# Half of w_out ahead of all other weight loads, a new order of loads, a weight product by halves, and value blocks on six banks: a fused attention and feed-forward kernel

## The chip, the cores and the metric

The kernel runs on one core of a Trainium2 chip. The metric is the device time of one execution in microseconds (us); the comparison is between medians of several executions. One execution of each kernel was also recorded by the hardware profiler. Its view has the engines TensorE (PE, with its weight loads as PEld), VectorE (DVE), ScalarE (ACT), GpSimd (POOL) and the queue engine SyncE (SP), and the DMA queues that move data between the chip's main memory and its on-chip memory.

## The reference, cut to what matters

Inputs are q, k, v of shape (8 batches, 12 heads, 448 positions, 64), two gain vectors g_q and g_k of 64, and the weights w1, w2 (768 x 1024), w3 (1024 x 1024) and w_out (1024 x 768), all float32.

```python
q_n, k_n = (rmsnorm(q, g_q), rmsnorm(k, g_k))
scores = scale * np.matmul(q_n, k_n.transpose(0, 1, 3, 2))
attn = softmax(scores)                     # written out in the original, with max and sum
attn_out = np.matmul(attn, v)
x = attn_out.transpose(0, 2, 1, 3).reshape(B * S, H * D)     # 3584 x 768
a = x @ w1
b = x @ w2
h = a * b @ w3
return h @ w_out                           # 3584 x 768
```

Nothing nonlinear stands between w3 and w_out, so the kernel forms w34 = w3 @ w_out once and multiplies a * b by it.

## The kernel before, in words

**Blocks.** The 96 heads are taken in 24 blocks of four heads; three blocks make a batch. Each block passes through the same steps. Its q and k (448 KB each) and v (four transfers) are loaded. ACT squares q and k (L414), DVE sums the squares (L421), ACT forms the inverse root (L430, L433), DVE scales (L444). The result is turned by TensorE transposes for the first five blocks (`do_turn`, L1049) and by DMA transposes for the others (L511). Seven score steps (`do_score`, L626) each fill two PSUM banks, and ACT's exponential (L648) empties them into P. Then the value step multiplies P by v and by ones (`start_pv`, `do_pv_main` L711, `do_pv_rest` L690), ACT inverts the sums (L733, L734), and DVE writes the scaled result xT (L753).

**Value blocks.** `pv_size` says whether one block or two are taken together. For two, the 64-row leftovers of both blocks are multiplied as pairs (L690, TensorE in tiles of 64 x 32), and the main part runs in tiles of 128 x 32 (L711). A double needs six PSUM banks in all, two for each of three kinds. It starts when `PV_BANKS` banks are free. The kinds that have both banks at the start take their leftovers first; the leftovers of the others come after the main part. While a double is due, `pe_try` starts no new score and no new pair.

**Pairs.** The feed-forward products and w34 are made by pairs of output tiles in two neighbouring PSUM banks (`Pair`, `do_pass`, L799), in TensorE tiles of 64 x 64: one pass is four matmuls that run side by side. In the first phase the upper 64 rows of each contraction chunk go to one bank and the lower to the other; in the second phase the row halves change places. Between the phases one engine relays a semaphore (`hand_over`), SP until all of w2 is loaded and POOL later, and another pair can run in the gap. At most `MAX_PAIRS` pairs are open. A w34 pair (L838) has 8 + 8 passes and needs one transposed tile of w3 (`do_w3_turn`, L1071) and both halves of w_out; eight such pairs make w34, 128 passes. A pair with w1 (f1a below) is copied to a_sb, one with w2 (f1b) is multiplied on DVE into abT (L882), and output pairs with w34 (f2) are copied to o_sb and stored (L938). The last tile is made by `do_last` (L991) and stored in four parts (L1005).

**Order.** A `Planner` written in the kernel keeps a clock of its own with assumed durations and lays down a fixed order for every engine while the program is built. On the chip each engine runs its list in that order and waits on semaphores. All weights and v, and q and k of blocks 1 to 5, are loaded by POOL in one list, `POOL_ORDER` (L253): w0 to w7 are eighths of w3, o0 and o1 halves of w_out, a0 to a2 thirds of w1, b0 to b2 thirds of w2, q1 to q5 the q and k of a block, v0 to v3 its v. The loads of one queue land in that order. At most eight are under way.

**The start.** `WARM` dummy matmuls (L1226) run first on TensorE. Then comes the product of the gains (`g_product`, L1239), four more dummies, and DVE spreads the gains (L1251, L1252) before it scales q and k of block 0. The planner takes TensorE as free from the value given at L1255.

Of the kernel before, what the change touches and what calls it, by code (L numbers as in the profile page):

```python
# [19 lines left out]
INF = float("inf")  # L20
SEM = 0.05
TO_ENGINE = 0.23
# [173 lines left out]
def kernel(  # L196
# [43 lines left out]

    N_PE_T = 5
    QUAD = 13.0
    WARM = 18
    MAX_PAIRS = 2
    MARGIN = 0.25
    LOW = 2
    PV_BANKS = 4
    SOON = 0
    AHEAD_W3 = 4
    EARLY = 4  # L250
    STOCK = 14
    PACE = 1.7
    POOL_ORDER = (  # L253
        "w0 w1 o0 w2 o1 q1 v0 w3 w4 q2 w5 v1 w6 w7 v2 a0 a1 a2 q3 b0 v3 b1 q4 b2 q5".split()
    )
    ON_POOL = (1, 2, 3, 4, 5)

# [510 lines left out]
    running = [None]  # L768

    class Pair:  # L770
        def __init__(self, name, nk, n, ready, sides, evacuate):
            self.name, self.nk, self.n = name, nk, n
            self.sides, self.evacuate = sides, evacuate
            self.phase, self.pos, self.gap_at = 0, 0, 0.0
            self.needs = ready

        def ready(self):
            return max(self.gap_at, self.needs(self.pos))

    def hand_over(p, mm, t):  # L780

        at = t + 0.23
        e = "SP" if max(w_at["w2"]) == INF else "POOL"
        nop = (nc.sync if e == "SP" else nc.gpsimd).nop()  # L784
        tc.add_manual_dep(
            nop.ins, mm.ins.name, SYNC_DEP, reason="first half of the sums complete"
        )
        free[e] = max(free[e], at)
        p.gap_at = free[e] + 0.15
        p.nop = nop  # L790

    def do_pass(p, t):
        took = pass_us(p.n) + into("n")
        first = None
        for r in range(2):
            z = r ^ p.phase
            lhsT, rhs = p.sides[z](p.pos)
            for h in range(2):
                mm = nc.tensor.matmul(  # L799
                    out=ps_all[64 * h : 64 * h + 64, p.bank + z, 0 : p.n],  # L800
                    lhsT=lhsT[64 * r : 64 * r + 64, 64 * h : 64 * h + 64],
                    rhs=rhs[64 * r : 64 * r + 64],
                    start=(p.phase == 0 and p.pos == 0),
                    stop=(p.phase == 1 and p.pos == p.nk - 1),
                    tile_position=(64 * r, 64 * h),
                    skip_group_check=True,
                )
                first = first or mm
        if p.phase == 1 and p.pos == 0:
            tc.add_manual_dep(  # L810
                first.ins, p.nop.ins.name, SYNC_DEP,
                reason="the other row half takes over the bank",
            )
        p.pos += 1
        running[0] = p
        if p.pos == p.nk:
            running[0] = None
            p.pos = 0
            p.phase += 1
            if p.phase == 1:  # L820
                hand_over(p, mm, t)
            else:
                pairs.remove(p)
                p.evacuate(p, t + took + TO_ENGINE - 0.187)
        return took

    def start_pair(p, z):
# [10 lines left out]
    def w34_pair(fc):  # L838
        def evacuate(p, at):
            z = p.bank  # L840

            def done(e):
                freed(z)(e)
                w34_at.append(e + SEM)

            add(
                None, {"ACT": 0.70, "DVE": 0.89}, -800.0,
                lambda e: copy_on(
                    e,
                    w34s[:, fc, :].rearrange("p (z n) -> p z n", z=2),  # L850
                    ps_all[:, z : z + 2, 0:NH],
                ),
                needs=[lambda: at], done=done,
            )

        side = lambda nh: lambda gc: (
            w3T[:, gc, fc * 128 : (fc + 1) * 128],
            w_outs[:, gc, nh * NH : (nh + 1) * NH],
        )
        return Pair(  # L860
            "w", CF, NH,
            lambda pos: max(w_at["w3T"][fc], w_at["w_out"][pos // (CF // 2)]) + SEM,
            (side(0), side(1)), evacuate,
        )

    a_sb = {}
# [112 lines left out]
    def do_last(t, z):  # L979


        x = last_x[0]
        last_x[0] += 1
        bp, tl = B // 2 - 1, NT - 1
        c0 = tl * 128 + HP * x
        w = NH // 2
        for fi in range(CF):
            for c in range(2):
                for nh in range(2):
                    n0 = nh * NH + c * w  # L990
                    nc.tensor.matmul(  # L991
                        out=ps_all[HP * nh : HP * nh + HP, z + c, 0:w],
                        lhsT=abT[bp][:, fi, c0 : c0 + HP],
                        rhs=w34s[:, fi, n0 : n0 + w],
                        start=(fi == 0), stop=(fi == CF - 1),
                        tile_position=(0, HP * nh), skip_group_check=True,
                    )
        took = 2 * CF * pass_us(w) + into("l")
        bank_at[z] = bank_at[z + 1] = INF
        o_sb = out_pool.tile([128, 2, NH], FP, tag="o_sb", name="o_sb")  # L1000
        ends = []

        def store(nh):
            eng = nc.scalar if nh and x else nc.sync
            eng.dma_start(  # L1005
                out=out_rows(bp, tl, x)[:, nh * NH : (nh + 1) * NH],
                in_=o_sb[HP * nh : HP * nh + HP, 0],
            )

        def done(e):  # L1010
            ends.append(e + SEM)
            if len(ends) == 2:
                for nh in range(2):
                    add(
                        "ACT" if nh and x else "SP", 0.6, -500.0 + nh,
                        lambda nh=nh: store(nh), needs=[lambda: max(ends)],
                    )

        for c, (e, us) in enumerate((("DVE", 0.27), ("ACT", 0.25))):
            add(  # L1020
                e, us, -500.0,
                lambda e=e, c=c: copy_on(
                    e, o_sb[:, 0, c * w : (c + 1) * w], ps_all[:, z + c, 0:w]
                ),
                needs=[lambda: t + took + TO_ENGINE_WIDE - 0.16], done=done,
            )
        return took
# [59 lines left out]
        return took  # L1087

    def next_pair(t):
        if len(pairs) >= MAX_PAIRS:  # L1090
            return None
        return next((p for p in waiting if p.ready() <= t), None)

# [61 lines left out]
    def pe_try(t, r):  # L1155
        idle = idle_banks(r)
        if pv_state:
            took = pv_state[0](t, idle)
            if took is not None:
                pv_state.pop(0)  # L1160
            return took
        size = pv_size(r)
        if mode[0] == "v" and len(idle) >= 1 and size == 1:
            return start_pv(t, 1, idle)
        if size == 2 and len(idle) >= PV_BANKS:
            return start_pv(t, 2, idle)
        two = adjacent(idle)
        score = score_ready(r) and out_scores[0] < 2 and two is not None and size != 2
        hungry = free["ACT"] <= t + 0.3 and out_scores[0] == 0
        if mode[0] == "t":  # L1170
            took = any_turn(t, r, idle, 1)
            if took is not None:
                return took
        if running[0] and running[0].ready() <= r:
            if score and hungry:
                return do_score(t, two)
            return do_pass(running[0], t)
        took = any_turn(t, r, idle, 2)
        if took is not None:
            return took  # L1180
        new = next_pair(r)
        late = [p for p in pairs if p.ready() <= r]
        if score:
            left = [z for z in idle if z not in (two, two + 1)]
            if hungry or late or new is None or adjacent(left) is not None:
                return do_score(t, two)
        if late:
            return do_pass(late[0], t)
        if size == 1 and len(idle) >= 2:
            return start_pv(t, 1, idle)  # L1190
# [17 lines left out]
    with tc.manual_schedule():  # L1208
# [22 lines left out]
        def g_product():  # L1231
# [13 lines left out]
                lhsT=gp_row.rearrange("a x d -> a (x d)"), rhs=ones_row[:, 0:1],  # L1245
                start=True, stop=True,
            )
            warm(4)

        def spread():  # L1250
            nc.vector.tensor_copy(out=g_b, in_=ps_all[:, 6, 0:D])  # L1251
            nc.vector.tensor_copy(out=g_col, in_=ps_all[:, 6, D : D + 1])  # L1252

        warm(WARM)
        free.update(ACT=4.0, DVE=4.0, SP=4.0, POOL=2.3, PE=7.6)  # L1255
        plan.now = plan.moved_to = 2.2
        plan.moving["SP"].append([2.3, 2.6, lambda t: None, 0.086])
        landed[0].update(q=4.5, k=5.4)
# [65 lines left out]
```

## Time and profile before

| | |
|---|---|
| median of 8 runs | 360.79 us (358.59 to 363.62) |
| the profiled execution | 358.59 us |
| its span | 356.8 us |
| time outside the span | 1.8 us |
| ACT, DVE busy | 261.5 us (73%), 207.7 us (58%) |
| first w3 transpose; first score matmul; first value block | 8.44; 11.51; 22.91 us |
| first pass with w1 | 53.09 us |
| start of the last matmuls (L991); last row on TensorE ends | 349.62; 352.45 us |
| granted TensorE clock in the rows | 1.00 throughout |
| bytes moved by DMA | 55.11 MB, mean 154 GB/s |

The profiled execution is the fastest of the eight. Times in the views count from the start of the span. A row of the timeline gives start, duration, engine, source line, operation, operands and count, and in brackets the idle time before it with what ended it. TensorE rows are pipelined: each row's duration contains a tail in which the next row already runs, so the pace is read from the distance between starts.

### The profile page before, as it was taken

The page shows a single profiled execution, that of the slowest core. Times are in us where ns is not written, and L with a number is a line of the kernel's source. Part 1 is how long each engine was busy: PE and PEld are TensorE (multiplying, and loading weights), DVE is VectorE, ACT ScalarE, POOL GpSimd, SP SyncE. Part 2 cuts the span into 40 slices and gives each one's busy share as a digit, 9 for nine tenths or more (in the row PEclk, how much of TensorE's full clock was granted, in tenths as well). Part 3 has the DMA queues.
Part 4 walks back from the last instruction along what each step waited for, and adds up shares of the span by engine and source line. Part 5 has one row for each costly group of instructions (what it writes and reads, how often), then busy time and mean ns, then how long its engine had stood idle before and what let it go on. Part 6 is the DMA issues. An engine that isn't in the chain of part 4 may idle for free.

```text
span 356.8 us, 16164 instructions
## 1 busy us (share of the span) xinstructions
PE 346.2 (97%) x7358; PEld 221.1 (62%) x7358; DVE 207.7 (58%) x293; ACT 261.5 (73%) x375; POOL 75.5 (21%) x132
## 2 busy tenths in 40 slices
PE   8699999999999999999999999999999999999994
PEld 3477656656665666656656565676665567666673
DVE  4278396997998797687579684465353330122200
ACT  4867978979997989988999899778686922222131
POOL 8168261314200505005031040500310000000000
PEclk9999999999999999999999999999999999999999
DMA  8999999679999899976799779961490005100046
GB/s 192 240 265 181 261 269 256 124 170 198 200 201 266 186 241 245 199 124 100 191 240 183 194 78 232 265 69 32 61 204 3 4 2 134 49 4 2 20 128 169
DMA packets 68360, 55.11 MB, mean 154 GB/s; under 512 B 44932, under 2 KB 62244, under 8 KB 68292
## 3 DMA queue, kind: packets, MB, share of 16 engines
q1 hardware_dynamic: 49904, 36.61, 44.6%
q0 software_dynamic: 18016, 16.92, 27.6%
q8 instruction: 57, 0.93, 1.1%
q10 hardware_dynamic: 372, 0.56, 0.5%
q14 instruction: 11, 0.09, 0.1%
HBM read 46.66 MB, written 11.01 MB: 162 GB/s over the span
## 4 chain that ended last, share of the span: by engine, by line
PE 73%; ACT 13%; DMA 6%; DVE 4%; issue 2%; POOL 1%; POOLq 0%; DVEq 0%; SPq 0%
PE ps_all L799 52%; PE ps_all L711 10%; PE ps_all L626 7%; ACT P L648 6%; DMA qk_sb<-in_q_dram 4%; PE ps_all L690 2%; ACT sq L414 2%; DMA qkT<-qks 2%; ACT Pr L648 1%; DVE qks L444 1%; DVE xT L753 1%; DVE ssq L421 1%; PE ps_all L991 1%; ACT w_outs L648 1%; ACT al L433 1%
## 5 line engine op out<-in xcount | busy, mean ns | idle before, releaser
L648 ACT ACTIVATE P<-ps_all 128x896 bf16<-128x896 f32 x120 | 105.1, 919 | 12.0 <-PE ps_all L626 11.8
L363 POOL DMA_DIRECT2D v_sb<-in_v_dram x96 | 57.4, 616 | 172.0 <-PE ps_all L799 118.4
L799 PE MATMUL ps_all<-xT,w2s 64*64 64x448 bf16 x1536 | 89.2, 349 | 0.3 <-ACT P L648 0.3
L799 PE MATMUL ps_all<-xT,w1s 64*64 64x448 bf16 x1536 | 89.4, 349 | 0.0
L799 PE MATMUL ps_all<-w34s,abT 64*64 64x384 bf16 x1728 | 79.3, 323 | 0.4
L882 DVE TENSOR_TENSOR abT<-ps_all,a_sb 128x896 bf16<-128x896 f32 x32 | 34.8, 1089 | 60.0 <-PE ps_all L799 51.4
L799 PEld LDWEIGHTS <-abT 64*64 64x64 bf16 x1728 | 52.4, 107 | 20.3 <-POOLq L784 1.6
L626 PE MATMUL ps_all<-qkT 64*64 64x448 bf16 x672 | 60.8, 352 | 2.9 <-ACT P L648 1.3
L799 PEld LDWEIGHTS <-w2s 64*64 64x64 bf16 x1536 | 47.5, 107 | 25.2 <-issue 1.6
L799 PEld LDWEIGHTS <-w1s 64*64 64x64 bf16 x1536 | 47.1, 107 | 25.1 <-issue 0.4
L421 DVE TENSOR_REDUCE ssq<-sq 128x14 f32<-128x896 f32 (+1 forms) x50 | 51.3, 1042 | 15.9 <-ACT sq L414 15.7
L444 DVE TENSOR_TENSOR qks<-qk_sb,al 128x448 bf16<-128x448 f32 x96 | 55.8, 618 | 4.6 <-ACT al L433 3.7
L414 ACT ACTIVATE sq<-qk_sb 128x896 f32<-128x896 f32 (+1 forms) x50 | 45.1, 918 | 4.8 <-DMA qk_sb<-in_q_dram 4.4
L753 DVE TENSOR_TENSOR xT<-ps_all,r 128x448 bf16<-128x448 f32 x48 | 28.1, 619 | 19.4 <-ACT r L734 18.4
L324 ACT ACTIVATE o_sb<-ps_all 128x768 f32<-128x768 f32 (+1 forms) x22 | 17.0, 771 | 27.8 <-PE ps_all L799 26.2
L324 ACT ACTIVATE a_sb<-ps_all 128x896 bf16<-128x896 f32 x20 | 18.3, 917 | 23.0 <-PE ps_all L799 23.0
L626 PEld LDWEIGHTS <-qkT 64*64 64x64 bf16 x672 | 21.5, 106 | 16.6 <-issue 5.8
L648 ACT ACTIVATE w_outs<-ps_all 128x896 bf16<-128x896 f32 x24 | 21.6, 915 | 8.5 <-PE ps_all L626 8.4
L711 PE MATMUL ps_all<-P,v_sb 128*32 128x448 bf16 x480 | 26.0, 352 | 0.0
L799 PE MATMUL ps_all<-w_outs,w3T 64*64 64x384 bf16 x512 | 24.5, 324 | 0.7 <-ACT P L648 0.5
L711 PEld LDWEIGHTS <-v_sb 128*32 128x32 bf16 x592 | 15.9, 97 | 12.1
L648 ACT ACTIVATE Pr<-ps_all 128x896 bf16<-128x896 f32 x24 | 22.1, 920 | 0.1
(60 smaller groups left out, 213.3 us busy)
## 6 DMA issues: line engine op xcount, KB each, us to landing
out_dram<-o_sb SPq DMA_DIRECT2D x54, 192.0 KB, 3.9
qk_sb<-in_q_dram SPq DMA_DIRECT2D x18, 448.0 KB, 5.0
qk_sb<-in_k_dram SPq DMA_DIRECT2D x18, 448.0 KB, 5.3
v_sb<-in_v_dram POOLq DMA_DIRECT2D x48, 64.0 KB, 4.5
v_sb<-in_v_dram POOLq DMA_DIRECT2D x48, 48.0 KB, 4.5
qk_sb<-in_q_dram POOLq DMA_DIRECT2D x5, 448.0 KB, 9.6
qk_sb<-in_k_dram POOLq DMA_DIRECT2D x5, 448.0 KB, 10.5
w3s<-in_moe_w_dram POOLq DMA_DIRECT2D x8, 256.0 KB, 5.9
```

What stands on the lines that cost most here:

```text
L324: nc.scalar.activation(out=out, in_=in_, func=AF.Copy, scale=1.0 if by is None else by)
L363: nc.gpsimd.dma_start(out=v_bufs[i % 4][p0 : p0 + HP, g::2, 0 : j1 - j0].rearrange("p h j d -> p h (j d)"), in_=src[:, g::2, j0:j1].rearra ...
L414: nc.scalar.activation(out=s["sq", t][:, x0:x1], in_=src[:, t, x0:x1], func=AF.Square)
L421: nc.vector.tensor_reduce(out=s["ssq"][:, t, x0:x1], in_=s["sq", t][:, x0:x1], axis=AX, op=ADD)
L444: nc.vector.tensor_tensor(out=s["qks"][:, t, :, x], in0=src[:, t, x], in1=s["alpha"][:, t, x].unsqueeze(2).broadcast_to([NP, NJ, D]), op=MULT,
L626: nc.tensor.matmul(out=sc[HP * c : HP * c + HP, u, 0:S].rearrange("p (j s) -> p j s", j=NJ), lhsT=qkT[u * D : (u + 1) * D, 1, j, cols], rh ...
L648: lambda: nc.scalar.activation(out=dst, in_=sc[:, :, 0:S], func=AF.Exp),
L690: nc.tensor.matmul(out=ps_all[hd * HALF : (hd + 1) * HALF, banks[x], 0:S], lhsT=(v_bufs[(i + x) % 4][g : g + HP, hd, NF, kind - 1 :: 2] if ...
L711: nc.tensor.matmul(out=ps_all[hd * HALF : (hd + 1) * HALF, z, 0:S], lhsT=value_weights(i, hd, j, kind), rhs=s["P"][:, hd, j, :] if j < NF ...
L753: lambda: nc.vector.tensor_tensor(out=xT[b][:, 2 * m + kind - 1, :], in0=ps, in1=s["r"], op=MULT),
L799: mm = nc.tensor.matmul(out=ps_all[64 * h : 64 * h + 64, p.bank + z, 0 : p.n], lhsT=lhsT[64 * r : 64 * r + 64, 64 * h : 64 * h + 64], rhs= ...
L882: nc.vector.tensor_tensor(out=abT[bp][:, f0 : f0 + 2, odd * S : (odd + 1) * S], in0=ps_all[:, z : z + 2, 0:S], in1=a_sb[b, f0], op=MULT,)
```

## The change

- `POOL_ORDER`: o0 moves from third place to first; w5 to w7 move behind a0 and v1, a1 and a2 come later, b0 ahead of a2, and b2 comes last.
- `Pair` has a list of steps in place of phase and position. With `halves=2` (the first three w34 pairs, `SPLIT`) it does both row assignments on the first half of w_out, then both on the second half, and changes rows twice in place of once.
- Until o1 is counted as landed, up to three pairs may be open (`EARLY_PAIRS`), and a single w3 tile may be transposed at once where two had to be ready.
- A double value block starts on six free banks in place of four.
- A score may break into a running pair earlier while few pairs are waiting (`STARVED`, `HUNGRY`, `ONE`).
- 15 + 1 dummy matmuls in place of 18 + 4; the planner's start value for TensorE goes from 7.6 to 7.2.
- The second half of every store of the last tile is issued by ACT; before, that was so for one of the two.

The engines' lists are laid down anew from all this. In the order of the built kernel, blocks 0, 1, 2 and 5 are taken singly, where before 0 and 5 were; doubles are ten in place of eleven, and every double has all its leftovers ahead of the main part.

```diff
-    WARM = 18
+    WARM = 15
...
-    PV_BANKS = 4
+    PV_BANKS = 6
     SOON = 0
+    STARVED = 6
+    HUNGRY = 0.9
+    ONE = 0
+    SPLIT = 3
+    EARLY_PAIRS = 3
...
-        "w0 w1 o0 w2 o1 q1 v0 w3 w4 q2 w5 v1 w6 w7 v2 a0 a1 a2 q3 b0 v3 b1 q4 b2 q5".split()
+        "o0 w0 w1 w2 o1 q1 v0 w3 w4 q2 a0 v1 w5 w6 v2 w7 a1 v3 q3 b0 a2 b1 q4 q5 b2".split()
...
-            self.phase, self.pos, self.gap_at = 0, 0, 0.0
-            self.needs = ready
+            self.k, self.gap_at, self.needs = 0, 0.0, ready
+            part = nk // halves
+            self.steps = [
+                (x ^ y, part * y + pos)
+                for y in range(halves) for x in range(2) for pos in range(part)
+            ]
...
+        swap, pos = p.steps[p.k]
         for r in range(2):
-            z = r ^ p.phase
-            lhsT, rhs = p.sides[z](p.pos)
+            z = r ^ swap
+            lhsT, rhs = p.sides[z](pos)
...
-            (side(0), side(1)), evacuate,
+            (side(0), side(1)), evacuate, 2 if fc < SPLIT else 1,
...
-            eng = nc.scalar if nh and x else nc.sync
+            eng = nc.scalar if nh else nc.sync
...
-        if len(pairs) >= MAX_PAIRS:
+        if len(pairs) >= (EARLY_PAIRS if w_at["w_out"][1] == INF else MAX_PAIRS):
...
-        hungry = free["ACT"] <= t + 0.3 and out_scores[0] == 0
+        low = sum(p.name != "w" for p in waiting) < STARVED
+        hungry = free["ACT"] <= t + (HUNGRY if low else 0.3) and out_scores[0] <= (
+            ONE if low else 0
+        )
...
-        took = any_turn(t, r, idle, 2)
+        took = any_turn(t, r, idle, 1 if w_at["w_out"][1] == INF else 2)
...
-            warm(4)
+            warm(1)
...
-        free.update(ACT=4.0, DVE=4.0, SP=4.0, POOL=2.3, PE=7.6)
+        free.update(ACT=4.0, DVE=4.0, SP=4.0, POOL=2.3, PE=7.2)
```

More of the change, by code (lines that the diff above doesn't have):

```diff
@@ L770, with __init__, changes @@
     class Pair:
-        def __init__(self, name, nk, n, ready, sides, evacuate):
-            self.name, self.nk, self.n = name, nk, n
+        def __init__(self, name, nk, n, ready, sides, evacuate, halves=1):
+            self.name, self.n = name, n
             self.sides, self.evacuate = sides, evacuate
-            self.phase, self.pos, self.gap_at = 0, 0, 0.0
-            self.needs = ready
-        def ready(self):
-            return max(self.gap_at, self.needs(self.pos))
+            self.k, self.gap_at, self.needs = 0, 0.0, ready
[4 more added lines that the diff above has]
+            ]
+        def ready(self):
+            return max(self.gap_at, self.needs(self.steps[self.k][1]))
+        def changes(self):
+            return 0 < self.k < len(self.steps) and (
+                self.steps[self.k][0] != self.steps[self.k - 1][0]
+            )
     def hand_over(p, mm, t):
@@ L802, in do_pass @@
                     rhs=rhs[64 * r : 64 * r + 64],
-                    start=(p.phase == 0 and p.pos == 0),
-                    stop=(p.phase == 1 and p.pos == p.nk - 1),
+                    start=(p.k == 0), stop=(p.k == len(p.steps) - 1),
                     tile_position=(64 * r, 64 * h),
@@ L808, in do_pass @@
                 first = first or mm
-        if p.phase == 1 and p.pos == 0:
+        if p.changes():
             tc.add_manual_dep(
@@ L813, in do_pass @@
             )
-        p.pos += 1
+        p.k += 1
         running[0] = p
-        if p.pos == p.nk:
+        if p.k == len(p.steps):
             running[0] = None
[L818 to L824, printed above, removed]
+            pairs.remove(p)
+            p.evacuate(p, t + took + TO_ENGINE - 0.187)
+        elif p.changes():
+            running[0] = None
+            hand_over(p, mm, t)
         return took
@@ L1014, in done @@
                     add(
-                        "ACT" if nh and x else "SP", 0.6, -500.0 + nh,
+                        "ACT" if nh else "SP", 0.6, -500.0 + nh,
                         lambda nh=nh: store(nh), needs=[lambda: max(ends)],
@@ L1168, in pe_try @@
         score = score_ready(r) and out_scores[0] < 2 and two is not None and size != 2
-        hungry = free["ACT"] <= t + 0.3 and out_scores[0] == 0
+        low = sum(p.name != "w" for p in waiting) < STARVED
+        hungry = free["ACT"] <= t + (HUNGRY if low else 0.3) and out_scores[0] <= (
+            ONE if low else 0
+        )
         if mode[0] == "t":
```

## The prediction

> **What bounds the kernel now.** I read the page's busy table first, then the chain of waits, then the timeline of TensorE where its starts are further apart than its work.
>
> ```profile
> PE 346.2 (97%) x7358; PEld 221.1 (62%) x7358; DVE 207.7 (58%) x293; ACT 261.5 (73%) x375; POOL 75.5 (21%) x132
> ```
>
> TensorE is near full by this table, but its rows contain pipeline tails, so I count work by pace. In the timeline, 20 matmuls with 448 columns (five passes) start at 236.49 and the next row at 237.44: 0.19 us a pass. A 384-column pass takes 0.1625 (8 passes from 127.33 to 128.76, less the drain of a tile change). Counted so, from the first transpose at 8.44 to the end of the last matmul at 352.45 there are 344.0 us, of which about 327.5 are work. Some 16.5 us are stalls, and only these and the start can give anything. The chain of waits agrees that the tail is pure TensorE and that ACT carries the chain from 55 to 105 us; its row at the start is a load:
>
> ```profile
> 5.49 14.15 DMA qk_sb<-in_q_dram
> ...
> 289.39 58.71 PE ps_all L799 x1324
> ```
>
> After the last double value block TensorE has 58.7 us of feed-forward with no wait. Attention ends early, so whatever TensorE saves earlier reaches the end, as long as attention keeps up. The largest stalls, in the timeline of TensorE:
>
> ```profile
> 7.43 0.20 PE L1239 MATMUL ps_all<-gp_row,ones_row 1*128 1x64 bf16 x1
> ...
> 11.51 0.95 PE L626 MATMUL ps_all<-qkT 64*64 64x448 bf16 x16 [0.79 <-DVE qkT L330]
> 12.92 1.65 PE L799 MATMUL ps_all<-w_outs,w3T 64*64 64x384 bf16 x32 [0.45 <-ACT P L648]
> 14.54 0.38 PE L626 MATMUL ps_all<-qkT 64*64 64x448 bf16 x4
> 15.35 0.38 PE L626 MATMUL ps_all<-qkT 64*64 64x448 bf16 x4 [0.43 <-ACT P L648]
> 16.16 0.38 PE L626 MATMUL ps_all<-qkT 64*64 64x448 bf16 x4 [0.43 <-ACT P L648]
> ```
>
> Four scores are 0.76 us of work and take 1.4 before the first w34 pass at 12.92 (the trace has o0 landing at 12.50). Then three scores take 2.4 us, paced by ACT: only half of w_out is there and nothing else is ready. A second place is at 80 us (whole timeline):
>
> ```profile
> 80.36 1.08 DVE L882 TENSOR_TENSOR abT<-ps_all,a_sb 128x896 bf16<-128x896 f32 x1
> 80.50 1.38 PE L626 MATMUL ps_all<-qkT 64*64 64x448 bf16 x15 [0.32 <-DVE xT L753]
> ...
> 81.89 1.33 PE L799 MATMUL ps_all<-w34s,abT 64*64 64x384 bf16 x28
> ```
>
> The first f2 tile needs the last f1b product, which DVE begins at 80.36 behind xT work; five scores (0.95 us) fill 79.64 to 81.89. The third is every double value block:
>
> ```profile
> 108.54 0.38 PE L690 MATMUL ps_all<-Pr,ones 64*32 64x448 bf16 x8
> ...
> 109.05 1.32 PE L711 MATMUL ps_all<-P,ones 128*32 128x448 bf16 x24
> ...
> 112.56 0.38 PE L690 MATMUL ps_all<-Pr,v_sb 64*32 64x448 bf16 x8
> 112.88 1.33 PE L799 MATMUL ps_all<-xT,w2s 64*64 64x448 bf16 x24
> ```
>
> From 112.56 to 112.88 two leftover passes, 0.19 of work, take 0.32: 0.13 for one change of tile form.
>
> **The change, part by part.** The sums compare the orders of the two built kernels, priced by these rows.
>
> *Start, up to the first value block.* Before, the gain product waits at 7.43 behind 18 dummies; DVE's copies start at 7.68 and its scaling at 7.88. Dummies are 0.217 apart when warm (four from 7.57 to 8.44), so three fewer let the product run near 6.8. DVE is then bound by its own sums, which end at 7.30, so scaling begins near 7.5, and first scores at about 11.15 in place of 11.51. The 16 w3 transposes that ran ahead (8.44 to 9.5) now fall between the scores, where there is room. The queue's first five weight loads are the same bytes in another order: landings before were w0 7.47, w1 8.73, o0 12.50, w2 13.76, o1 17.54; with o0 first I work out o0 near 10, w0 11.25, w1 12.5, and w2, o1 and q1 as before. Seven exponentials at 0.83 from 11.6 end near 17.4, so the last score starts near 16.3. In the gaps there is 1.6 of transposes and 11 w34 passes (1.8), all on o0. Then 37 passes, 6.0 us, end near 22.3, with o1 there since 17.5. Before, the value block began at 22.91 with 40 passes done; now 48 are. Gain: 0.6 + 8 x 0.1625 = 1.9. I take 1.8 (bounds 0.8, if w0 or w1 land a microsecond late with scores queued behind their transposes in TensorE's list, and 2.2). The extra row changes are three more relays on SP, each about 0.4 us; with three pairs open another runs meanwhile: nothing (1.1 if uncovered). SP has only first loads queued then. w3T copies move from ACT to DVE, idle 6.2 us there.
>
> *23 to 55 us.* q1 lands at 19.6 in either order, so block 1 starts no sooner. Later w5 to w7 (to about 36.7), a1 (39) and a2 (47.5) come 1 to 2 us ahead of their first use by this count: nothing, with up to 1 us against. Blocks 1 and 2 taken singly cost 2 x 2.38 (the single from 22.91 to 25.29) in place of 4.20 (47.12 to 51.32): +0.56. Ten more changes between transposes and 64 x 64 tiles: the Trainium skill (TensorEngine Tiling (Array Packing), Key Properties) says that any change of tiling mode drains the array, which speaks against this shredding. The rows price it unequally: about 0.1 going in (three passes at 33.14, next row at 33.73), nothing coming out (24 transposes end near 36.1, scores start at 35.99). Five of the pairs lie in the score-paced start: +0.3. By the rule at one price both kernels have the same number of changes, since ten doubles lose one each, and the sum would be nil; by the rows the two differ. The last w34 pairs of before lose 0.76 between 44.4 and 47.1 with nothing to put in the relay gap; now value blocks and f1a lie there: -0.5 (bounds 0 and -0.76).
>
> *Around 80 us.* In the new order a double stands between the last f1b and the first f2, so the DVE product is covered by 4 us of work: -1.2 (bounds 0 and -1.3).
>
> *Doubles.* Ten save one change: -1.3. The six free banks cost a wait. At each double at most the last pair's two banks are still held; the pair before it ended one phase, 1.14 us, earlier, and needs 0.2 to reach its engine and 0.92 (ACT) or 1.09 (DVE) to be copied: short by up to 0.2. One double has its last score only six passes ahead. With ACT busy the wait is longer. I take 0.15 each, +1.5 (bounds nil and 4).
>
> *Earlier scores and the last stores.* Scores only exchange places with passes: nothing, 0.5 either way. SP's third store of the last tile is issued at 353.26 behind two others; with one fewer ahead the end comes 0.2 sooner (bounds -0.3, +0.1, since ACT's issue of 0.54 stands ahead of its last copy).
>
> *Fewer dummies.* From about 7.3 to 11.2 TensorE would now have 1.2 us of work in 3.9. The Trainium skill (TensorE: Matmul & The Clock Gate, Part 1: The HAM clock gate) has the array at half clock until it was busy for some 3.4 us, and again after an idle window of that length. The trace agrees on the first half: dummies are 0.427 apart until about 5.4 and 0.217 after, though the granted-clock row says 1.00. If the thin stretch counted as idle, 3.4 us at half rate would cost up to 1.7. The nearest row is 12.92 to 16.96, with 1.9 of work in 4.0 us, after which passes run at full pace. I take nothing; the case is a rival.
>
> **Sum.** -1.8 + 0.56 + 0.3 - 0.5 - 1.2 - 1.3 + 1.5 - 0.2 = -2.6. On the profiled execution (span 356.8 and 1.8 around it, 358.59) that gives 356.0. That one is the fastest of eight, 2.2 under their median of 360.79, so the median becomes **358.2 us**.
>
> **Rivals.**
> 1. *The wait for six banks decides (slower).* While a double is due neither scores nor pairs start, so if the closing pair's copy queues behind an exponential on ACT, TensorE stands. For: ACT busy 9.9 of 10 us from 80 to 100, copies 0.92. Against: one phase of other work covers most of it. Without this term the sum is -4.1, so it decides from 0.41 us a double; at 0.75, 364.2.
> 2. *Attention sets the pace.* TensorE's lead waits at the next value block, since ACT's work is the same. For: the chain on ACT from 55 to 105. Against: TensorE hardly stalled there, and ACT idles some 3 of 20 us from 100 to 120. The start's 1.8 is given back: 360.0.
> 3. *The clock falls in the thin start*: 1.5 of the start's gain is lost: 359.7.
>
> **How the numbers follow.** My forecast 0.52, rival 1 0.17, rival 2 0.22, rival 3 0.09. A measurement of this kernel can tell about 0.5% (1.8 us) from no change. The forecast is faster by 0.7%; its own bounds run from 355.5 (start 2.2, no bank wait) to 361. Of its cases most are faster; rivals 2 and 3 lie within 0.5%, save their edges. Faster 0.54, within 0.29, slower 0.17. The range reaches from 355.3 to part of rival 1's cases, 362.3; above lies most of the rest.
>
> **What would show it.** Right: first score near 11.2, w34 passes without a pause after the third transpose, the first value block near 22.3 with 48 passes behind it, no score-only stretch before the first f2, doubles without L690 rows after the main part. Wrong: TensorE gaps ahead of the first L690 row of doubles, naming ACT or DVE (rival 1); the first f2 of a batch at the old time in spite of an earlier start (rival 2); passes near 11 to 15 us at twice their spacing (rival 3).

## The result, and the profile after

| | before | after |
|---|---|---|
| median | 360.11 us (357.85 to 363.66, 57 runs) | 356.97 us (354.85 to 358.71, 20 runs) |
| ratio of the runs | | 0.9908, 95% interval 0.989 to 0.9927 |
| profiled execution, span | 358.59, 356.8 us | 356.08, 354.3 us |
| first score; first value block | 11.51; 22.91 us | 11.04; 23.98 us |
| w34 passes done at the first value block | 40 | 48 |
| start of the last matmul; from there to the end of the span | 352.20; 4.60 us | 349.42; 4.88 us |
| mean granted clock of the profiled execution | 1.000 | 0.992 |

The change makes the kernel 0.9% faster, and the interval does not reach 1. The prediction said 0.7% faster, 358.2 us. It stands 1.2 us above the measured median; 0.7 of that is only that the kernel before has a lower median over 57 runs (360.11) than over the eight known then (360.79). The total is near, but partly by luck: two of its terms were wrong by about 1.5 us each in opposite directions.

First the page's busy table of the kernel after, to be read against the one of before. TensorE is as full as before; ACT has 5 us less and DVE 6 us more, because seven instructions moved from one to the other (ACT 375 to 368, DVE 293 to 300).

```profile
PE 343.3 (97%) x7352; PEld 223.3 (63%) x7352; DVE 213.4 (60%) x300; ACT 256.2 (72%) x368; POOL 75.4 (21%) x132
```

In the chain of waits (start, duration, what) the end is again pure TensorE, beginning 0.06 us from where it began before and 2.4 us shorter, since 60 matmuls fewer are left by then:

```profile
5.48 13.25 DMA qk_sb<-in_q_dram
...
289.33 56.30 PE ps_all L817 x1264
```

The timeline of TensorE from the gain product to the first value block:

```profile
6.36 0.18 PE L1257 MATMUL ps_all<-gp_row,ones_row 1*128 1x64 bf16 x1 [0.46 <-DVE gp_row L1250]
...
6.48 0.39 PE L1244 MATMUL ps_all<-warm_t 128*128 128x512 bf16 x1
8.68 0.56 PE L1064 MATMUL ps_all<-ident,qks 128*128 128x128 bf16 x7 [1.81 <-DVE qks L449]
9.75 0.56 PE L1064 MATMUL ps_all<-ident,qks 128*128 128x128 bf16 x7 [0.51 <-DVE qks L449]
11.04 0.96 PE L631 MATMUL ps_all<-qkT 64*64 64x448 bf16 x8 [0.72 <-DVE qkT L335]
11.93 1.03 PE L1086 MATMUL ps_all<-ident,w3s 128*128 128x128 bf16 x8
12.89 0.96 PE L631 MATMUL ps_all<-qkT 64*64 64x448 bf16 x8
...
17.52 6.53 PE L817 MATMUL ps_all<-w_outs,w3T 64*64 64x384 bf16 x148
23.98 0.75 PE L716 MATMUL ps_all<-P,ones 128*32 128x448 bf16 x12
```

The gain product is early and the first score is at 11.04, a tenth from the 11.15 worked out. But eight score matmuls then take 0.89 us from start to start (11.04 to 11.93), where two score steps are 0.38, and eight transposes 0.96. The stretches of the same time, with granted clock (the column behind POOL), show why:

```profile
9.00:10.00 1.00, 0.49 (x10) 0.32 (x8) 1.00 (x3) 0.00 (x0) 0.00 (x0) 1.00 1.16 215
10.00:11.00 1.00, 0.32 (x6) 0.14 (x3) 0.92 (x2) 0.00 (x0) 0.61 (x1) 0.84 1.10 207
11.00:12.00 1.00, 0.96 (x9) 0.26 (x10) 0.00 (x0) 0.33 (x1) 0.36 (x1) 0.50 1.18 219
12.00:13.00 1.00, 1.00 (x12) 0.80 (x16) 0.00 (x0) 1.00 (x2) 0.33 (x2) 0.50 1.08 196
13.00:14.00 1.00, 1.00 (x11) 0.29 (x12) 0.69 (x1) 0.86 (x2) 0.50 (x1) 0.50 1.18 215
14.00:15.00 1.00, 1.00 (x24) 0.74 (x22) 0.43 (x1) 1.00 (x2) 0.58 (x1) 0.95 1.15 209
```

The clock is at one half for 0.32 + 3 + 0.1 = 3.4 us, just when the transposes and first scores come. This is rival 3. Around 80 us the double stands where the score-only stretch was, and the first f2 tile follows it without a wait:

```profile
77.32 2.44 PE L716 MATMUL ps_all<-P,v_sb 128*32 128x448 bf16 x48
79.69 0.38 PE L631 MATMUL ps_all<-qkT 64*64 64x448 bf16 x4
79.91 0.98 PE L817 MATMUL ps_all<-w34s,abT 64*64 64x384 bf16 x20
```

And a double, in the timeline of TensorE:

```profile
108.94 1.30 PE L817 MATMUL ps_all<-xT,w1s 64*64 64x448 bf16 x24
110.17 0.38 PE L695 MATMUL ps_all<-Pr,ones 64*32 64x448 bf16 x8
110.37 0.56 PE L695 MATMUL ps_all<-Pr,v_sb 64*32 64x448 bf16 x16
110.87 1.32 PE L716 MATMUL ps_all<-P,ones 128*32 128x448 bf16 x24
112.01 2.44 PE L716 MATMUL ps_all<-P,v_sb 128*32 128x448 bf16 x48
114.38 0.38 PE L631 MATMUL ps_all<-qkT 64*64 64x448 bf16 x4
```

All leftovers (L695) stand ahead of the main part. Six f1a passes from 108.94 are 1.14 of work and the leftovers start at 110.17: 0.09 more, a change of tile form and nothing else. There is no wait for six banks.

### The profile page after: what moved, and what is told of

Same layout as the page of the kernel before. It is cut to its first block, busy times and chain, and to the rows that moved or that the text cites. A ratio compares the mean times of both kernels' runs of the same rounds, so it can differ in the third digit from the quotient of the medians.

```text
span 354.3 us, 16130 instructions
## 1 busy us (share of the span) xinstructions
PE 343.3 (97%) x7352; PEld 223.3 (63%) x7352; DVE 213.4 (60%) x300; ACT 256.2 (72%) x368; POOL 75.4 (21%) x132
## 3 DMA queue, kind: packets, MB, share of 16 engines
HBM read 46.66 MB, written 11.01 MB: 163 GB/s over the span
## 4 chain that ended last, share of the span: by engine, by line
PE 84%; DMA 6%; ACT 5%; DVE 1%; POOL 1%; issue 1%; SPq 0%; DVEq 0%; POOLq 0%; ACTq 0%
PE ps_all L817 61%; PE ps_all L716 11%; PE ps_all L631 8%; DMA qk_sb<-in_q_dram 5%; PE ps_all L695 2%; ACT w_outs L653 1%; ACT P L653 1%; ACT sq L419 1%; PE ps_all L1064 1%; DMA out_dram<-o_sb 1%; ACT a_sb L329 1%; POOL w3s L397 0%; DVE qks L449 0%; PE ps_all L1086 0%; POOL w_outs L403 0%
## 5 line engine op out<-in xcount | busy, mean ns | idle before, releaser
L817 PE MATMUL ps_all<-w34s,abT 64*64 64x384 bf16 x1728 | 80.7, 323 | 0.0
L631 PE MATMUL ps_all<-qkT 64*64 64x448 bf16 x672 | 62.0, 357 | 1.6 <-ACT w_outs L653 0.8
L817 PEld LDWEIGHTS <-w1s 64*64 64x64 bf16 x1536 | 48.7, 107 | 23.4 <-issue 0.4
L329 ACT ACTIVATE a_sb<-ps_all 128x896 bf16<-128x896 f32 x22 | 20.2, 919 | 30.0 <-PE ps_all L817 30.0
L335 DVE COPY o_sb<-ps_all 128x768 f32<-128x768 f32 (+1 forms) x16 | 14.1, 881 | 32.9 <-PE ps_all L1006 15.8
L631 PEld LDWEIGHTS <-qkT 64*64 64x64 bf16 x672 | 22.7, 107 | 15.1 <-issue 5.8
L329 ACT ACTIVATE o_sb<-ps_all 128x768 f32<-128x768 f32 (+1 forms) x15 | 11.2, 747 | 23.7 <-PE ps_all L817 22.0
```

What stands on the lines that cost most here:

```text
L329: nc.scalar.activation(out=out, in_=in_, func=AF.Copy, scale=1.0 if by is None else by)
L335: nc.vector.tensor_copy(out=out, in_=in_)
L631: nc.tensor.matmul(out=sc[HP * c : HP * c + HP, u, 0:S].rearrange("p (j s) -> p j s", j=NJ), lhsT=qkT[u * D : (u + 1) * D, 1, j, cols], rh ...
L817: mm = nc.tensor.matmul(out=ps_all[64 * h : 64 * h + 64, p.bank + z, 0 : p.n], lhsT=lhsT[64 * r : 64 * r + 64, 64 * h : 64 * h + 64], rhs= ...
```

## The experiments

Medians and ratios to the kernel before, which ran beside each on the same chip. The medians of different groups come from different chips, so the ratios compare better. e1, e2, e8, e9 and e10 rest on five or six runs each, e11 on one.

| kernel | median, us | ratio, 95% interval |
|---|---|---|
| the changed kernel | 356.97 | 0.9908 (0.989 to 0.9927) |
| e1: nine dummies behind the gain product | 354.72 | 0.9861 (0.9836 to 0.9886) |
| e2: four free banks | 362.7 | 1.0082 (1.0053 to 1.0112) |
| e3: the kernel before with six free banks | 359.63 | 0.9992 (0.9973 to 1.0012) |
| e4: old loads, no halves, 16 dummies | 361.28 | 1.0023 (0.9997 to 1.0049) |
| e5: e1 without earlier scores | 357.76 | 0.9931 (0.9911 to 0.9951) |
| e6: e1, third kind of leftovers behind | 359.67 | 0.9998 (0.9979 to 1.0017) |
| e7: e1 with the old load order | 359.29 | 0.9997 (0.9966 to 1.0027) |
| e8: e1 without halves | 355.54 | 0.9878 (0.9842 to 0.9914) |
| e9: eleven dummies ahead and eleven behind | 354.77 | 0.9836 (0.9794 to 0.9878) |
| e10: e9 with the old last stores | 354.62 | 0.9845 (0.9803 to 0.9888) |
| e11: e7 once more, one profile | 358.83 | |

Below, "lead" is how much sooner than in the kernel before a matmul starts that has the same amount of TensorE work ahead of it, counted at the paces of the prediction; the leftovers of a block taken singly are counted at a double's pace, so that what single blocks cost shows as lost lead.

**e1, the clock.**

```diff
-            warm(1)
+            warm(9)
```

> The changed kernel with nine dummy matmuls in place of one after the gain product; no other instruction moves. Theory 1 (the thin start let TensorE's clock fall to half for 3.4 us, which ate the start's gain): granted clock 1.00 throughout, first value block near 22.3 in place of 23.98, and about 355.2 us, the level of those runs of the changed kernel whose mean clock was 1.000 (354.64, 355.42, 355.68), some 1.8 under its median. Rival (attention sets the pace, a lead at the start is given back): the clock is full and the first value block earlier, but the time stays within 0.5 us of 357.0.

Measured 354.72 us, 2.2 less than the changed kernel by the medians and 1.7 by the ratios, and the mean clock was 0.997 or more in every execution, with TensorE's order otherwise the same. That is outside the rival's half microsecond around 357.0. The rows of the start in e1's profile, at full pace from the first transposes on:

```profile
7.49 0.20 PE L1257 MATMUL ps_all<-gp_row,ones_row 1*128 1x64 bf16 x1
...
7.63 2.12 PE L1244 MATMUL ps_all<-warm_t 128*128 128x512 bf16 x9
9.58 1.21 PE L1064 MATMUL ps_all<-ident,qks 128*128 128x128 bf16 x14
11.51 0.57 PE L631 MATMUL ps_all<-qkT 64*64 64x448 bf16 x8 [0.72 <-DVE qkT L335]
12.01 0.62 PE L1086 MATMUL ps_all<-ident,w3s 128*128 128x128 bf16 x8
```

The first value block is at 23.29, not near 22.3 as theory 1 had it, in part since the first score is later (11.51 in place of 11.04).

The changed kernel's 21 recorded executions (one more than the table's 20) fall into three sorts by their mean clock: six at 0.997 and above average 355.6 us, eight between 0.992 and 0.995 average 356.6, seven at 0.990 and below 357.7. A window of 3.4 us at half clock in a span of 354 takes 0.005 from the mean. After TensorE's last matmul the clock falls as well (from 352.02 on in the profile of the changed kernel), which takes about 0.003 more and delays no matmul. So the three sorts are none, one and two windows, and each window costs about 1.05 us. The median of all 21 lies about 1.4 us above that of the six without a window. That every window lies in the start is not shown: only a profile shows where one lies. The kernel before has such executions too, 14 of the 38 beside e1 at 0.995 and below, though its one profile shows no window. With nine fillers behind the gain product and o0 first (e1, e5, e6, e8) none of 53 executions has one; with the changed kernel's start it is 15 of 21. e1 is also 0.3 us (by the ratios) to 0.8 us faster than the changed kernel's executions without a window; that part is not explained.

**e2 and e3, the six banks alone.** e2 is the changed kernel with the first line, e3 the kernel before with the second:

```diff
-    PV_BANKS = 6
+    PV_BANKS = 4

-    PV_BANKS = 4
+    PV_BANKS = 6
```

> The changed kernel with doubles starting on four free banks again. Theory 2 (most of the gain comes from six banks: one tile change less in each of ten doubles, and the double that covers the DVE product near 80 us): back to about 359.5 us, a lead over the kernel before of under 1 us. Rival (loads and halves bring the gain): 357.3.

> The kernel before with six free banks for doubles and nothing else; its order up to the first product with w2 is the old one. Theory 2: about 357.5 us, the 1.3 at 80 us and 1.2 from the doubles gained, no L690 row after the main part. The forecast's first rival (the wait for six banks costs more than the tile change saves): 360 or more, with gaps ahead of the first leftover row of doubles. If loads and halves bring the gain: 360.

e2 is slower than the kernel before (362.7 us), and slower than either expectation, 359.5 and 357.3. e3 is the same as the kernel before (359.63), so theory 2's 357.5 missed. In e2 the cover at 80 us is gone: from TensorE's and the other engines' timeline,

```profile
80.04 0.55 PE L631 MATMUL ps_all<-qkT 64*64 64x448 bf16 x4
80.08 2.08 DVE L897 TENSOR_TENSOR abT<-ps_all,a_sb 128x896 bf16<-128x896 f32 x2
80.86 1.19 PE L631 MATMUL ps_all<-qkT 64*64 64x448 bf16 x12 [0.27 <-ACT P L653]
...
82.21 0.38 PE L631 MATMUL ps_all<-qkT 64*64 64x448 bf16 x4 [0.16 <-DVE abT L897]
82.47 0.84 PE L817 MATMUL ps_all<-w34s,abT 64*64 64x384 bf16 x16
```

and TensorE waits there 1.5 us again. In e3 that wait is gone and a lead of 1.1 appears, but other score-only stretches give it back: 2.0 us in three pieces between 89 and 99 us and 1.9 ahead of the first f2 tile at 119 to 122. The doubles of e3 take 4.21 us each, as in the changed kernel, where nearly all of those before take 4.33 or 4.34. So six banks do what the prediction said at 80 us and within the doubles, and in the old order the gain is lost again elsewhere. Of e2's loss 1.4 us are stops of TensorE within a product, at 103 and 153 us, like those of e11 below; the rest is spread over its order and is not traced.

**e4, the change without its loads and halves.**

```diff
-    SPLIT = 3
-    EARLY_PAIRS = 3
+    SPLIT = 0
+    EARLY_PAIRS = 2
...
-        "o0 w0 w1 w2 o1 q1 v0 w3 w4 q2 a0 v1 w5 w6 v2 w7 a1 v3 q3 b0 a2 b1 q4 q5 b2".split()
+        "w0 w1 o0 w2 o1 q1 v0 w3 w4 q2 w5 v1 w6 w7 v2 a0 a1 a2 q3 b0 v3 b1 q4 b2 q5".split()
...
-        took = any_turn(t, r, idle, 1 if w_at["w_out"][1] == INF else 2)
+        took = any_turn(t, r, idle, 2)
```

> The changed kernel with the old order of loads, no halves, two open pairs at the start and two w3 tiles before a transpose step; the dummies stay at 15 + 1, but 16 w3 transposes now fill the stretch from 8 to 9 us again. Theory 1: the clock stays at 1.00 and the time is 356.5 to 357.2, no worse than the change, since its start gained only 0.3 us net of the clock. Rival (loads and halves bring the gain): 359 or more.

Measured 361.28 us: theory 1 missed, the rival's 359 or more holds. Six banks and earlier scores without the loads and halves are not faster than the kernel before. Its profile has waits of 1.3 us at 81 and 1.5 at 123, in stretches with nothing but scores. It also stands for 0.9 and 0.8 us at 97 and 104 in the middle of a product and of a score with no wait that the profile shows, as in e11. The gain does not fall into parts that add up.

**e5 to e8, one part each taken out of e1.**

e5:

```diff
-    STARVED = 6
+    STARVED = 0
```

> The changed kernel with the nine filling dummies (354.7 us) and the earlier-scores rule switched off; everything else as in it. Theory (the edits only work together: double value blocks that use up both free banks and pairs need scores issued early enough to keep pairs in stock): stretches of scores with no pair waiting come back between 80 and 125 us, as when six banks were put alone into the kernel before; about +2, 356.5 to 357.5 us, and the lead over the kernel before at equal TensorE work falls by about 2 us from 70 to 125 us. Rival (the prediction's own view: scores only exchange places with passes): 354.2 to 355.2 us.

Measured 357.76 us, a little above the interval that the theory gave, and the interval of its ratio does not touch that of e1. Its lead falls from 2.1 at 84 us to 0.4 at 102 us, and to nothing by 124 us. So, with the new order that comes with them, the earlier scores, to which the prediction gave nothing, are worth 2.5 us (by the ratios) to 3 us (by the medians).

e6:

```diff
-        firsts = range(min(3, len(idle) // 2) if size == 2 else 0)
+        firsts = range(2 if size == 2 else 0)
```

> The changed kernel with the filling dummies, where a double value block still opens on six free banks but takes only two of its three kinds of leftover in its first tile form, so that the third comes behind the main part with its own change of form, as before. Theory (one change of form costs the 0.13 us of the trace): ten changes, +1.3, so about 356.0 us, with rows of two leftover passes behind each main part of a double. Rival (the change of form is hidden by a wait for the banks that ends at the same time): 354.5 to 355.0 us, with a gap of 0.1 to 0.2 us ahead of the first row of each double in its place. Passes and scores may come in another order behind the first double, which can move either figure by 0.5.

Measured 359.67 us. Both numbers fall: it costs 4.9. Nearly all doubles take 4.33 us where the changed kernel's take 4.21, so ten changes of form are 1.2 of it, as the theory had them; the rest is the order behind the first double, which changed as well and has stretches with nothing but scores, as e3 and e5 have. Ten microseconds from 90 on, first e1, then e5, then e6 (busy us of PE, PEld, DVE, ACT, POOL):

```profile
90.00:100.00 10.00, 10.00 (x224) 6.52 (x220) 9.29 (x14) 7.51 (x11) 2.38 (x4) 1.00 1.08 236
```

```profile
90.00:100.00 10.00, 9.03 (x188) 6.10 (x182) 5.55 (x7) 9.87 (x15) 2.37 (x4) 1.00 0.94 230
```

```profile
90.00:100.00 10.00, 9.40 (x196) 5.79 (x192) 5.28 (x7) 9.94 (x15) 2.38 (x4) 1.00 1.33 243
```

In e1 TensorE is covered and DVE is the busier one; in the two others ACT is full with exponentials, DVE stands half idle, and TensorE issues fewer matmuls (188 and 196 in place of 224). Feed-forward products feed DVE, scores feed ACT: the orders that lose bring many scores together in this stretch. This is rival 2's mechanism, attention setting the pace, in one place and only in orders that run out of pairs.

e7:

```diff
-        "o0 w0 w1 w2 o1 q1 v0 w3 w4 q2 a0 v1 w5 w6 v2 w7 a1 v3 q3 b0 a2 b1 q4 q5 b2".split()
+        "w0 w1 o0 w2 o1 q1 v0 w3 w4 q2 w5 v1 w6 w7 v2 a0 a1 a2 q3 b0 v3 b1 q4 b2 q5".split()
```

> The changed kernel with the filling dummies and the old order of loads: w0 and w1 ahead of o0, a0 behind w7. Halves, six banks and earlier scores stay. Theory (o0 first is what the early weight products wait for): o0 lands at 12.5 in place of 10.1 us, the first score stretch has fewer passes to lay between its scores, the first value block starts with about 40 passes done in place of 48: +1.0 to +1.5, 355.7 to 356.2 us. Rival (the start is paced by ACT's exponentials and the halves alone, loads come early enough in either order): 354.5 to 355.2 us.

Measured 359.29 us, more than either said. Its first value block is at 23.32 with 48 passes done, not about 40 (23.31 in e11), against 22.46 to 23.29 in the kernels with o0 first and a full clock (e1, e5, e6, e9, e10), so the order of loads is worth between nothing and 0.9 us at the start. The rest is lost after 125 us, in another order and in the stops of e11 below; how much lies in each is not separated.

e8:

```diff
-    SPLIT = 3
-    EARLY_PAIRS = 3
+    SPLIT = 0
+    EARLY_PAIRS = 2
```

> The changed kernel with the filling dummies and the new load order, but no weight product is split by halves of w_out and only two pairs are open early. Theory (with half of w_out there and whole products only, two pairs run out of passes after o0's half and TensorE stands until o1 lands at 17.6 us): the first value block starts with fewer passes done, stalls between scores from 14 to 18 us as before: +1.0 to +2.0, 355.7 to 356.7 us. Rival (load order alone carries the start): 354.5 to 355.2 us.

Measured 355.54 us, between the two; its interval overlaps that of e1. The stall is there, as the theory had it:

```profile
15.68 0.91 PE L631 MATMUL ps_all<-qkT 64*64 64x448 bf16 x8
17.64 5.39 PE L817 MATMUL ps_all<-w_outs,w3T 64*64 64x384 bf16 x128 [1.06 <-DMA w_outs<-in_moe_w_out_dram]
```

TensorE waits for o1, and the lead at the first value block is 0 where e1, e5, e6, e9 and e10 have 1.0 to 1.8. At the end its profiled execution has a lead of 3.3, within 0.7 of e9's 4.0. So the halves are worth 1.0 to 1.8 us at the start, and only about 0.8 of it is seen in the medians; where the rest is lost is not shown.

**e9 and e10, the start and the last stores.**

```diff
-    WARM = 15
+    WARM = 11
...
-            warm(1)
+            warm(11)
```

> The changed kernel with eleven dummies ahead of the gain product and eleven behind it (15 and 1 in the changed kernel, 15 and 9 in the run with nine filling dummies); the order of everything else is the same. Theory (the gap ahead of the first transposes let the clock fall, and the gain product itself no longer waits for dummies but for DVE): granted clock 1.00 throughout, first score at 11.0 to 11.5 us, 354.0 to 354.9 us, no better than with nine fillers by more than 0.5. Rival (the dummies that stand ahead of the gain product still delay the start, as the prediction had it): first score 0.5 us sooner than with nine fillers and 353.9 to 354.4 us; if the stretch still counts as idle, passes at half pace near 11 to 14 us and about 356.

Measured 354.77 us; its order is the changed kernel's. The theory holds for the time. The first score is at 10.68, 0.8 sooner than in e1's profile, which the rival had said, but the median doesn't show it. One reason why the profiles of the start differ lies ahead of the gain product. The distance between dummies drops from 0.43 to 0.22 us at a time that varies between executions: after 6 slow dummies in the changed kernel's profile, 12 in that of the kernel before, 15 in e1. In e1 all dummies ahead of the gain product were slow, and it ran at 7.49 us; in e9 it ran at 6.00. So the prediction's 0.217 us for each dummy left out was not a fixed price. e9's timeline at full clock:

```profile
10.68 0.57 PE L631 MATMUL ps_all<-qkT 64*64 64x448 bf16 x8 [0.72 <-DVE qkT L335]
11.18 0.62 PE L1086 MATMUL ps_all<-ident,w3s 128*128 128x128 bf16 x8
...
22.46 0.75 PE L716 MATMUL ps_all<-P,ones 128*32 128x448 bf16 x12
```

Eight scores now take 0.50, and the first value block comes at 22.46; the prediction had 22.3. But e10, whose list for TensorE is the same, has its first score at 11.01 and its first value block at 23.10.

e10 is e9 with:

```diff
-            eng = nc.scalar if nh else nc.sync
+            eng = nc.scalar if nh and x else nc.sync
...
-                        "ACT" if nh else "SP", 0.6, -500.0 + nh,
+                        "ACT" if nh and x else "SP", 0.6, -500.0 + nh,
```

> As the run with eleven and eleven dummies, with the old split of the last stores: SP issues three of the last tile's four, ACT one, and ACT's list has no store between its last two copies. TensorE's list is the same in both. Theory (ACT's 0.54 us of issue ahead of its last copy delays the last store as much as SP's shorter queue speeds it up): from the last row of the last matmul line to the end of the span the old split takes 4.2 to 4.6 us, as before, against 4.64 in the changed kernel; the time is the same or 0.3 lower. Rival (the prediction's term): 0.2 us longer than with the new split.

Measured 354.62 us. From the start of the last matmul to the end of the span it takes 4.79 us (4.83 in e9). Over all profiles the old split gives 4.61 to 5.08, the new one 4.55 to 5.09. The split of the stores is worth nothing that these profiles can tell.

**e11, stops without a wait.**

> A second look at the kernel with the old load order. Its first profile has TensorE standing for 3.1 us in the middle of one f1a product, from 147.4 to 150.7, with no wait that the profile shows, while the queue that carries instructions had a gap of 9.4 us between two blocks. Theory (TensorE's instructions came late because other transfers filled the queues, which varies from execution to execution): the stall at this place is gone or of another size, and stalls without a wait over 0.5 us stand only where that queue has a gap of 8 us or more. Rival (an order of this kernel's own work makes it wait there): 2.5 to 3.5 us at the same matmul.

The same rows of TensorE's timeline, first in e7's profile and then in e11's:

```profile
146.68 0.95 PE L817 MATMUL ps_all<-xT,w1s 64*64 64x448 bf16 x16
150.68 0.57 PE L817 MATMUL ps_all<-xT,w1s 64*64 64x448 bf16 x8 [3.06 <-issue]
...
153.37 2.22 PE L817 MATMUL ps_all<-xT,w1s 64*64 64x448 bf16 x24
155.42 1.30 PE L817 MATMUL ps_all<-xT,w2s 64*64 64x448 bf16 x24
```

```profile
145.59 0.95 PE L817 MATMUL ps_all<-xT,w1s 64*64 64x448 bf16 x16
147.38 0.57 PE L817 MATMUL ps_all<-xT,w1s 64*64 64x448 bf16 x8 [0.84 <-issue]
```

Here "issue" stands where the profile shows nothing that TensorE waited for. The stop is at the same point of the same product, between the sixteenth and the seventeenth of its 24 matmuls; its size fell from 3.06 to 0.84 us. A second place does the same: 1.12 us at 51.68 in e7, 0.30 at 50.84 in e11. The theory's first half holds (another size). Its second half doesn't: this is e11's only stop over 0.5 us without a named wait, and it follows a gap of 7.7 us between two blocks on the instruction queue, not of 8. Nor is a long gap enough: the kernel before has one of 9.0 us, from 76.2 to 85.2, and no such stop. That late instruction fetch causes the stop is a reading which fits place and size, and is not shown.

The stop costs more than itself. In e7 the granted clock is one half for 3.4 us from 151.80 on, just behind it: the six passes from 153.37 take 2.05 us to the next row where the six from 155.42 take 1.23. So a window at half clock need not come from the start.

## Why the prediction was right, point by point

| step | predicted | measured in the profiled pair |
|---|---|---|
| start, to the first value block | -1.8 | -0.2; at full clock -0.9 to -1.75, mean -1.3 |
| clock in the thin start (part of the -0.2) | 0 (rival 3: 1.5) | +0.7 to +1.5, mean +1.1 |
| 23 to 55 us | +0.36 | about +0.5, counted to 75 us |
| around 80 us | -1.2 | -1.3 to -1.5 |
| ten doubles, one change of form less | -1.3 | -1.2 |
| ten doubles, wait for six banks | +1.5 | 0 |
| earlier scores | 0 | needed: 2.5 to 3.0 without them (e5) |
| last stores | -0.2 | nothing (+0.3 in this pair) |

*Start.* The kernel before begins its value block at 22.91 with 40 passes done; with 48 it would be 22.91 + 8 x 0.1625 = 24.21. The five profiles at full clock with o0 first and halves (e1, e5, e6, e9, e10) are there at 23.29, 22.95, 22.77, 22.46 and 23.10. That is a gain of 0.9 to 1.75, in the mean 1.3: inside the bounds, smaller than the 1.8 taken. The changed kernel is there at 23.98 (e2, whose clock fell too, at 24.00), 0.7 to 1.5 later than the five and 1.1 in the mean, close to the 1.05 that a window costs; rival 3 said 1.5. The step that failed is "I take nothing" for fewer dummies. I chose by the nearest row, 1.9 us of work in 4.0, after which the passes kept full pace. From the last dummy at 6.48 to the first score at 11.04 there were two groups of seven transposes, about 1 us of work in 4.6: half as dense as that row. The work of the thin stretch was transposes, that of the other row passes and scores; whether it is the density that counts, and where its limit lies, no run shows. Here the rule that I cited against the row, from the Trainium skill (TensorE: Matmul & The Clock Gate, Part 1: The HAM clock gate), was the better guide: the half clock lasted 3.4 us, its window, although the stretch before wasn't idle but thin.

*23 to 55 us.* In the changed kernel the lead goes from 0.27 at the first value block to -0.26 at 75 us; in the five full-clock profiles it falls by 0.5 to 0.9. That is somewhat more than the 0.36 worked out, and the runs don't split it into single blocks, changes of form and relay gaps. One sum in that part is a slip: there are five more changes into transposes and five more out of them, and two of the five pairs lie in the start, not five; the other three at 0.1 make the +0.3. Rival 2 would have all of the start's lead given back; at full clock 0.1 to 1.0 us of it is left at 75 us, and in e1, e9 and e10 the lead then grows to 2.8 to 4.0 us at the last matmul.

*Around 80 us.* The lead goes from -0.26 at 75 us to about 1.2 at 85. In e2, with four banks, this step is missing, and in e3, with six in the old order, it is there. The mechanism was right and so was its size. The gain lasts only where the next stretch with nothing but scores is covered too: the changed kernel still has one at 117.25, 1.3 us of waiting ahead of the first f2 tile.

*Doubles.* The saving was right. The wait of 0.15 us for six banks was not there: in all ten the idle time ahead of the first L695 row is 0.10 to 0.13 us, the same as ahead of the doubles of before. I had summed phase 1.14 against 0.2 + 0.92 or 1.09, short by up to 0.2; what took up that shortage isn't shown; the tile change, 0.1 us that I had counted apart, lies at the same moment. Rival 1, which rested on this wait, falls.

*Earlier scores.* "Scores only exchange places with passes" failed. In the order with them TensorE and DVE stay covered between 84 and 124 us, where e5 without them loses its lead.

*The sum.* Two large errors cancelled, and that is luck: +1.5 for a wait that wasn't there, and -1.8 for a start that gave -0.2, of which the clock, put at nothing, is 1.1 and the size of the gain 0.5. The measured rows make -0.2 + 0.5 - 1.4 - 1.2 + 0.3 = -2.0 of the pair's 2.5 us; the other 0.5 lies in single waits between 85 and 110 us that I have not tied to one edit.

*What stays open.* Each part taken out changes the planner's whole order, so e2 and e4 to e8 measure the part together with a new order, and in e2, e4 and e7 with stops of TensorE as well. The runs show that the parts need each other, and where the losing orders stand. They don't show why the planner falls into these orders.

## What to carry to other kernels

When early work is thinned out or moved forward, look at what TensorE does in the few microseconds ahead of it: keep fillers in the gap, behind what the next engine waits for. That was worth about 2 us here, against 3.1 for the whole change. Fewer fillers ahead of it made no difference to the median (e9 against e1). Where a planner lays out the order, cost a part by what stands in each stretch of the new order: taken alone six banks gave nothing (e3), and four banks in the changed kernel, with the order that came of it, cost 5.7 us (e2).

## What the runs showed of the hardware that I had not expected

- A stretch with about 1 us of matmul work in 4.6 was thin enough for the granted clock to fall to 0.50 for 3.4 us, though not in every execution: six of 21 have no such window by their mean clock. One window cost about 1.05 us of the execution.
- The dummies' first change from 0.43 to 0.22 us apart came between 3.7 and 7.6 us into the span over the thirteen profiles.
- TensorE can stop for 0.8 to 3.1 us within a product with no wait that the trace shows, at the same matmul in two executions of the same kernel (e7, e11). e1's profile has one of about 0.9 us at 222 us, within a value block, and e10's one of 0.8 at the same value block. Behind the stop of 3.1 us the clock fell to 0.50 for 3.4 us.
